# Cumulative log-decays of an RWKV-7 chunk by VectorE transposes and scans instead of TensorE products

## The chip, the core and the metric

One core of one Trainium2 chip runs the kernel. The metric is the device time of one execution in microseconds; a kernel's time is the median over its runs. Engines are TensorE (PE in the profile, its weight loads PEld), VectorE (DVE), ScalarE (ACT), GpSimd (POOL) and SyncE (SP), whose queue issues nearly all DMA transfers.

## The reference

An RWKV-7 recurrence feeds a two-layer MLP with exact GELU.

```python
B, H, S, D = 4, 8, 768, 40                    # r, k, v, w, a, b: (B, H, S, D) float32
for t in range(S):
    y[:, :, t] = einsum('bhd,bhde->bhe', r_t, state)
    Sa = einsum('bhde,bhe->bhd', state, a_t)
    state = state * w_t[:, :, None, :] - outer(Sa, b_t) + outer(v_t, k_t)
x = y.transpose(0, 2, 1, 3).reshape(3072, 320)
out = gelu_exact(x @ w_in) @ w_out            # w_in 320 x 2048, w_out 2048 x 320, float64 in memory
```

## The kernel before

**Chunks.** The 768 steps are cut into 12 chunks of 64 tokens. In a chunk the recurrence is written with matrix products: the decays enter through cumulative products of `w` along the tokens, which are exponentials of cumulative sums of `log w`. All 32 heads are worked at once, as two halves (`g`) and four pairs (`i` or `n`) on the 128 partitions. Work of several chunks overlaps: while the state of chunk c is computed, the inputs of c+1 are prepared, the MLP of an earlier chunk fills TensorE, and GpSimd inverts a triangular matrix.

**The steps of a chunk**, by the names that stand in the order:

- Loads: `Lw`, `La`, `Lb`, `Lk`, `LV`, `Lr`, with tokens on the partitions, and from the third or fourth chunk on `La`, `Lv`, `Lr`, `Lbt`, `Lkt` in pairs of tokens (`load_pairs`), a form that VectorE's 32x32 transposes (`turn`) bring into the layout with features on the partitions. `Lv` and, for chunk 1, `Lr` load `v_pairs`; `La` and `Lbt` share `a_pairs`, `Lr` and `Lkt` share `r_pairs`.
- Decays: `lg` takes the logarithm of `w` in place (ScalarE). `wT` multiplies it on TensorE by the lower triangular matrix `cum_m` so that cumulative sums come out in a PSUM bank with features on the partitions (32 products; the profile shows 64 records, since every product of float32 operands appears as two). `ew` writes exp of these sums to `wpT`, `en` exp of their negative to `kT`. `cu` and `ec` do the same with tokens on the partitions: `ec` writes exp of the negative sums to `part`, which `sb` (VectorE) multiplies into `b` and `sk` (GpSimd for most chunks) into `k`.
- Preparation: `ta`, `tb`, `tk`, `tv`, `tr` transpose; `sa` multiplies `aT` by `wpT`, `sn` makes `nT` from `b` and `kT`, and `kc` then overwrites `kT` with the scaled `k`. So `kT` holds first `en`'s result and later the operand that `am` reads.
- Small products: `nm`, `am`, `vm` on TensorE, masked by `nk`, `ak`, `vk` on VectorE.
- Block inverse (chunk 0 on TensorE by `qm` steps, the others on GpSimd): `Ns` stores the matrix to `N_blocks` in DRAM, `Nl` loads it to `Nb` in another layout, `ic` is 62 instructions of GpSimd on `W`, `Is` stores to `inv_blocks`, `If` and `Ij` load the result to `Tt` and `T2`; `tc_`, `jm`, `jc`, `km`, `kt0`, `kt1` join the blocks.
- State: `av`, `xm`, `xc0`, `xc1`, `sm`, `sc`, `pk`, `pb`, `oa`, `om`, `od`, `ym`, `yc`, `oc`, `tm`, `tn`. `om` writes the rows for the MLP to `xt`, and `ox` moves some of them between partitions by DMA.
- MLP: `mh` (eight parts) and `ge` (GELU); `pm` and `pc`, or from chunk 3 on seven products `m1` to `m7` of a Strassen form with sums `s1` to `s4`, `e1` to `e6`, then `so` stores.
- At the start the float64 weights are loaded (`Lf`, `Lf5`, `Ls`) and turned into float32 by `cp`, `cm`, `cs`, `ce`, `cv` and, in some units, `cl`, `cn`, `cg` (or `cx`, `cy`). `warm` steps are products without use of their result.

**Order.** Nothing is scheduled by the framework. `order` returns one list of step names, and each engine and each DMA queue works its own instructions in the order of that list, waiting on semaphores where data or buffers ask for it. TensorE's results go through four PSUM tiles of two banks each (`take`, `bank`, `drop`): a step waits until the tile that it takes was dropped and read.

Of the kernel before, what the change touches and what calls it, by code (L numbers as in the profile page):

```python
# [16 lines left out]
def order(chunks, first_seven):  # L17
    return """
        pads_a.1 pads_a.0 Lw.0 Lf.0.1.0 lg.0 warm_set identity sums_mask first_ones.1 warm.4.20 warm_first
        Lf.0.0.0 pads_w.1 bias_set pads_r.0 pads_extra.2 pads_extra.3 first_ones.0 pads_rows.1 pads_w.0  # L20
        pads_extra.0 pads_rows.0 upper_mask pads_r.1 iz.1 pads_extra.1 cm.0 cn.0 wT.0 warm.4.5 cu.0 ec.0 cl.0
        cx.0 ew.0 Lf.1.1.0 Lf.1.0.0 Lb.0 La.0 sb.0 cp.1 tb.0 cp.0 ce.0 sn.0 ta.0 sa.0 nm.0 Lw.1 Lb.1 Lf.2.1.0
        Lf5.0.1 Lf.2.0.0 ce.1 lg.1 cm.1 nk.0 qi cu.1 wT.1 warm.4.29 ec.1 cs.0 cy.0 qt qm.0 cs.1 sb.1 cp.2 cm.2
        La.1 qc.0 Lf5.0.0 Lf.3.0.0 cn.2 ew.1 cl.4 ce.2 cl.2 qz.0 Lf.3.1.0 Lf.0.0.1 ta.1 tb.1 warm.4.7 qm.1 cv.1
        sa.1 cp.3 cm.3 sn.1 cs.2 qc.1 qz.1 qa.1 Lr.0 nm.1 tr.0 warm.4.24 LV.0 Lk.0 cg.2 pads_VR.0 Tt_zero sk.0.p
        nk.1 cm.4 qm.2 tv.0 tk.0 Lf.0.1.1 rc.0 ce.3 cs.3 cp.4 qa.2 cv.3 qc.2 cl.5 cn.4 kc.0 qz.2 qm.3 cm.5 cp.5
        cn.5 ce.5 cs.5 ce.4 vc.0 am.0 vm.0 qz.3 qa.3 ak.0 Lf5.1.1 Lf.2.1.1 Lf.2.0.1 Lf.1.1.1 Lw.2 Lf.1.0.1 Ns.1.1
        Ns.1.0 Lk.1 cg.5 pads_VR.1 cs.4 cg.4 cp.7 cm.7 vk.0 qc.3 lg.2 ce.7 cl.7 cn.7 qm.4 cp.6 qa.4 ql ce.6 cm.6
        sk.1.v cs.7 av.0 Lf5.1.0 Nl.1.1 Lr.2 Nl.1.0 Lr.1 Lf.3.0.1 Lf.3.1.1 LV.1 Ls.1 Lb.2 Ls.0 qx warm.4.8 jm.0
        jc.0 cu.2 km.0 xc0.0 cg.7 cs.6 xc1.0 cp.9 cm.9 kt0.0 ce.9 kt1.0 cs.9 cv.9 tr.2 ec.2 rc.2 sm.0 sc.0.0  # L30
        sc.0.1 tk.1 pk.0 pb.0 cv.6 cp.8 kc.1 ce.8 wT.2 tr.1 om.0.0 om.0.1 od.0.0 od.0.1 cm.8 cm.11 cs.8 cv.8 sb.2
        cp.11 tv.1 rc.1 vc.1 ew.2 am.1 vm.1 ak.1 vk.1 cp.10 oc.0 ce.11 cm.10 cs.11 tm.0 tn.0 tb.2 warm.4.1 ox.0.0
        av.1 ym.1 ce.10 sn.2 yc.1 La.2 ta.2 cs.10 cv.10 cv.11 sa.2 Ls.2 Ls.3 cp.12 cp.13 cm.13 cm.12 LV.2 Ls.5
        xm.1 nm.2 tv.2 ox.0.1 Ls.4 Ls.7 Ls.9 Ls.6 Ls.11 nk.2 Ls.8 ic.1.0.4 ic.1.4.8 ic.1.8.12 ic.1.12.16
        ic.1.16.20 ic.1.20.24 unused.v ic.1.24.28 ic.1.28.31 Ns.2.0 Is.1.0.s ce.12 ce.13 cs.13 cv.13 cp.15 cm.15
        xc0.1 ce.15 vc.2 xc1.1 cs.12 cs.15 cv.12 cv.15 cp.17 cm.17 cm.14 ce.17 cn.14 cl.14 cp.14 ce.14 cs.17
        cv.17 cp.19 cm.19 cs.14 cg.14 ce.19 cs.19 cv.19 cp.21 cm.21 Ns.2.1 Ls.13 Is.1.1.s mh.0.6 mh.0.2 mh.0.3
        ge.0.1 mh.0.0 mh.0.1 mh.0.7 mh.0.4 mh.0.5 cp.16 cm.16 ce.21 cs.21 ge.0.0 cn.16 ce.16 cl.16 cv.21 cp.23
        cm.23 cs.16 ce.23 cs.23 cg.16 cv.23 Ls.15 cm.25 cn.25 cl.25 cm.18 cp.25 ce.25 cp.18 cs.25 iz.2 cg.25
        Nl.2.1 If.1.1 vm.2 Ls.10 If.1.0 Ij.1.1 Ij.1.0 Nl.2.0 Ls.12 vk.2 ce.18 pm.0.0 unused.a ic.2.0.4 ic.2.4.8  # L40
        ic.2.8.12 ic.2.12.16 ic.2.16.20 ic.2.20.24 ic.2.24.28 ic.2.28.31 tc_.1 jm.1 jc.1 km.1 cs.18 cv.18 cp.20
        cm.20 ce.20 cs.20 cv.20 cp.22 Ls.14 Lk.2 Lw.3 kt1.1 unused.r kt0.1 ce.22 ge.0.2 cs.22 cm.22 cv.22 ge.0.3
        cp.24 sk.2.v pm.0.1 sm.1 warm.4.0 tk.2 sc.1.1 sc.1.0 pk.1 pb.1 lg.3 kc.2 oa.1.1 oa.1.0 od.1.0 om.1.1
        cm.24 od.1.1 cu.3 ec.3 ce.24 cs.24 om.1.0 cv.24 wT.3 am.2 ak.2 La.3 Lr.3 Lv.3 Lb.3 pm.0.2 tm.1 ew.3 oc.1
        tn.1 av.2 ym.2 yc.2 pm.0.3 ta.3 tr.3 sa.3 sb.3 pc.0.0 pc.0.1 tb.3 xm.2 ox.1.1 Lw.4 ox.1.0 sn.3 nm.3 Lk.3
        so.0.1 tv.3 nk.3 Is.2.0.s Is.2.1.s Ns.3.1 Ns.3.0 sk.3.v Lk.4 Nl.3.1 If.2.0 If.2.1 Ij.2.0 Nl.3.0 Ij.2.1
        mh.1.6 mh.1.4 mh.1.7 ge.1.3 xc0.2 mh.1.5 lg.4 ge.1.2 mh.1.0 mh.1.1 ge.1.0 xc1.2 mh.1.2 tc_.2 jm.2 jc.2
        tk.3 km.2 mh.1.3 kc.3 kt1.2 kt0.2 ge.1.1 sm.2 Lv.4 La.4 sc.2.0 pk.2 wT.4 sc.2.1 ta.4 pb.2 oa.2.0 oa.2.1
        om.2.1 od.2.1 od.2.0 om.2.0 Lr.4 Lbt.4 Lb.5 pm.1.0 am.3 vm.3 ew.4 en.4 oc.2 tb.4 tr.4 sn.4 ak.3 vk.3 sa.4
        pm.1.1 pm.1.3 tm.2 pc.1.1 LV.3 ox.2.1 so.0.0 ox.2.0 cu.4 nm.4 pm.1.2 nk.4 iz.3 ic.3.0.4 ic.3.4.8  # L50
        ic.3.8.12 ic.3.12.16 ic.3.16.20 ic.3.20.24 ic.3.24.28 ic.3.28.31 Is.3.1.p Is.3.0.p ec.4 sk.4.p iz.4
        so.1.1 Lkt.4 tk.4 kc.4 pc.1.0 Ns.4.1 Ns.4.0 Lb.4 Nl.4.1 Nl.4.0 If.3.1 La.5 If.3.0 Ij.3.1 tc_.3 tn.2
        mh.2.6 mh.2.7 mh.2.4 ge.2.3 mh.2.5 ge.2.2 av.3 ym.3 yc.3 mh.2.2 mh.2.3 jm.3 xm.3 ge.2.1 Lw.5 Ij.3.0 jc.3
        km.3 xc0.3 kt0.3 tv.4 xc1.3 ta.5 kt1.3 mh.2.0 mh.2.1 sm.3 Lr.5 ge.2.0 so.1.0 Lbt.5 tr.5 vm.4 vk.4 sb.4
        sc.3.0 sc.3.1 tb.5 pm.2.0 am.4 pk.3 pb.3 ak.4 oa.3.0 oa.3.1 om.3.1 ws.0 om.3.0 od.3.1 od.3.0 lg.5 wT.5
        en.5 sn.5 ew.5 sa.5 Lkt.5 Lv.5 LV.5 La.6 LV.4 ox.3.1 pm.2.1 pm.2.2 tm.3 nm.5 pm.2.3 nk.5 pc.2.1 pc.2.0
        oc.3 tn.3 av.4 ym.4 yc.4 ic.4.0.4 ic.4.4.8 ic.4.8.12 ic.4.12.16 ic.4.16.20 ic.4.20.24 ic.4.24.28
        ic.4.28.31 Is.4.1.p Is.4.0.p ox.3.0 Ij.4.1 If.4.1 If.4.0 Ns.5.1 so.2.1 Ij.4.0 mh.3.0 cu.5 xm.4 tv.5 tk.5
        kc.5 tc_.4 ec.5 jm.4 mh.3.1 jc.4 xc0.4 km.4 kt0.4 ge.3.0 mh.3.6 mh.3.7 Ns.5.0 so.2.0 Nl.5.1 xc1.4 Nl.5.0
        Lw.6 Lr.6 ge.3.3 lg.6 kt1.4 ta.6 sm.4 sc.4.0 ws.3 Lv.6 Lbt.6 sc.4.1 tr.6 mh.3.2 pk.4 pb.4 mh.3.4 mh.3.5  # L60
        mh.3.3 ws.1 oa.4.0 oa.4.1 om.4.1 om.4.0 Lkt.6 iz.5 ic.5.0.4 ic.5.4.8 ic.5.8.12 ic.5.12.16 ic.5.16.20
        ic.5.20.24 ic.5.24.28 ic.5.28.31 Is.5.1.p Is.5.0.p ge.3.1 ge.3.2 vm.5 wT.6 am.5 ox.4.1 m1.3 m2.3 vk.5
        s1.3 ws.2 od.4.0 ak.5 en.6 e1.3 s2.3 od.4.1 tk.6 oc.4 ew.6 e2.3 tb.6 m5.3 m6.3 e4.3 s3.3 tm.4 tn.4 e3.3
        av.5 ym.5 yc.5 sn.6 s4.3 kc.6 sb.5 sa.6 m3.3 m7.3 m4.3 e5.3 e6.3 nm.6 nk.6 xm.5 cu.6 Lb.6 ox.4.0 La.7
        Lk.5 Lr.7 sk.5.p If.5.1 ec.6 mh.4.0 If.5.0 so.3.1 Ns.6.1 Ij.5.0 tr.7 xc1.5 tv.6 ta.7 tc_.5 Ij.5.1 Ns.6.0
        Nl.6.1 Nl.6.0 Lbt.7 mh.4.2 mh.4.1 ge.4.0 mh.4.3 jm.5 mh.4.4 mh.4.5 jc.5 xc0.5 km.5 ge.4.2 kt0.5 ge.4.1
        kt1.5 mh.4.6 sm.5 vm.6 sc.5.1 sc.5.0 vk.6 mh.4.7 ge.4.3 s1.4 pk.5 pb.5 LV.6 Lw.7 Lk.6 Lv.7 Lkt.7 so.3.0
        m1.4 m2.4 tb.7 oa.5.0 oa.5.1 om.5.0 om.5.1 od.5.0 s2.4 s4.4 tk.7 m5.4 lg.7 e1.4 ox.5.1 am.6 wT.7 m6.4
        e2.4 one_set s3.4 od.5.1 e4.4 ak.6 ew.7 en.7 m3.4 m7.4 tm.5 oc.5 e3.4 tn.5 iz.6 ic.6.0.4 ic.6.4.8
        ic.6.8.12 ic.6.12.16 ic.6.16.20 ic.6.20.24 ic.6.24.28 ic.6.28.31 Is.6.1.p Is.6.0.p sk.6.p m4.4 sn.7 sa.7  # L70
        e5.4 e6.4 nm.7 av.6 ym.6 sb.6 nk.7 tv.7 ox.5.0 Lr.8 tr.8 yc.6 mh.5.4 cu.7 ec.7 Ns.7.0 so.4.1 Ns.7.1
        If.6.1 If.6.0 Ij.6.0 so.4.0 Nl.7.0 xm.6 vm.7 mh.5.5 vk.7 kc.7 xc1.6 tc_.6 mh.5.6 mh.5.7 mh.5.0 ge.5.3
        jm.6 mh.5.1 Ij.6.1 Nl.7.1 ge.5.2 jc.6 xc0.6 km.6 ge.5.0 kt0.6 mh.5.2 kt1.6 sm.6 sc.6.0 sc.6.1 Lw.8 La.8
        ta.8 mh.5.3 Lkt.8 ge.5.1 lg.8 pk.6 pb.6 s1.5 m5.5 s4.5 oa.6.0 oa.6.1 om.6.1 s2.5 wT.8 am.7 m1.5 m2.5
        od.6.0 om.6.0 ak.7 e3.5 e1.5 s3.5 LV.7 Lv.8 Lb.7 Lbt.8 Lk.7 iz.7 ic.7.0.4 ic.7.4.8 ic.7.8.12 ic.7.12.16
        ic.7.16.20 ic.7.20.24 ic.7.24.28 ic.7.28.31 Is.7.1.p Is.7.0.p sk.7.p m6.5 ox.6.1 m3.5 m7.5 tb.8 en.8 sn.8
        e2.5 od.6.1 e4.5 ew.8 oc.6 tm.6 tn.6 sb.7 e5.5 av.7 ym.7 yc.7 m4.5 sa.8 tv.8 e6.5 Lb.8 ox.6.0 LV.8 Lk.8
        La.9 cu.8 vm.8 ec.8 vk.8 xm.7 nm.8 If.7.1 Ij.7.1 Ij.7.0 nk.8 tk.8 xc1.7 kc.8 Ns.8.0 Ns.8.1 If.7.0 Nl.8.1
        Nl.8.0 tc_.7 mh.6.6 mh.6.7 ge.6.3 xc0.7 mh.6.4 mh.6.0 jm.7 mh.6.5 jc.7 km.7 mh.6.1 mh.6.2 kt0.7 ge.6.2
        so.5.1 Lw.9 kt1.7 ta.9 sm.7 sc.7.0 sc.7.1 ge.6.0 lg.9 mh.6.3 cu.9 pk.7 pb.7 ge.6.1 Lr.9 so.5.0 Lbt.9 Lv.9  # L80
        tr.9 s1.6 oa.7.1 sb.8 om.7.1 oa.7.0 m1.6 m2.6 s2.6 s3.6 om.7.0 s4.6 od.7.0 iz.8 sk.8.p ic.8.0.4 ic.8.4.8
# [38 lines left out]
def kernel(  # L120
# [16 lines left out]
    C = 64  # L137
# [1202 lines left out]
```

## Time and profile before

| | before |
|---|---|
| three runs | 690.76, 685.67, 688.01 us, median 688.01 |
| the profiled execution | 684.3 us, its span 682.6 us |
| TensorE products | 652.3 us busy, 96% |
| VectorE | 385.2 us, 56% |
| GpSimd | 377.2 us, 55% |
| ScalarE | 236.9 us, 35% |
| DMA | 74.26 MB in 286043 packets, 265660 of them under 512 bytes |
| granted TensorE clock, mean | 0.989 |

The span runs from the first to the last instruction on the engines. The page cuts it into 40 slices of 17 us and gives the busy tenths of each engine; matmul ends are modelled. A row of a group gives the line, the engine, the operation, the tiles written and read, the shapes and the number of records, then busy time and mean duration in ns, then the time that the engine stood idle just before them and what ended most of it. In an answer by windows the five busy times stand in the order PE, PEld, DVE, ACT, POOL, then the granted clock, the DMA share and GB/s. A row of waits gives who waited for whom: microseconds in total, times, the longest.

### The profile page before, as it was taken

The numbers are of one execution on the slowest core, as the hardware profiler recorded it, in microseconds if no ns is written. First come the engines' busy times: TensorE is split into PE (matmuls) and PEld (weight loads), VectorE is DVE, ScalarE is ACT, GpSimd is POOL, SyncE is SP. The second block draws the span as 40 slices with busy tenths as digits, with TensorE's granted clock in tenths as the row PEclk, the third lists the DMA queues.
The fourth block names the chain that finished last, engine by engine and source line by source line (L and its number), as shares of the span: only waits on it lengthen the run. The fifth ranks groups of instructions, "written<-read, shape, count | busy, mean of one in ns | idle before, by whom it ended". The sixth has DMA issues, their size and how long they took to land.

```text
span 682.6 us, 29596 instructions
## 1 busy us (share of the span) xinstructions
PE 652.3 (96%) x13250; PEld 569.6 (83%) x13250; DVE 385.2 (56%) x483; ACT 236.9 (35%) x313; POOL 377.2 (55%) x796
## 2 busy tenths in 40 slices
PE   8687999999999999999989989999999999999997
PEld 4476887788778778998988988997998998998987
DVE  1868989750833645781852853753952763624403
ACT  4547535526222325322323332432342332132020
POOL 3445854853857705871883874864873863840000
PEclk9987999999999999999999999999999999999999
DMA  9987668758668746458547766656767153140100
GB/s 157 161 163 161 129 165 176 131 97 145 111 127 126 150 82 125 95 102 129 110 83 138 126 118 120 129 95 125 131 123 142 35 100 68 31 71 16 26 15 21
DMA packets 286043, 74.26 MB, mean 109 GB/s; under 512 B 265660, under 2 KB 280796, under 8 KB 285916
## 3 DMA queue, kind: packets, MB, share of 16 engines
q1 hardware_dynamic: 284852, 69.84, 55.2%
q0 software_dynamic: 864, 2.36, 2.0%
q8 instruction: 104, 1.70, 1.1%
q14 instruction: 23, 0.19, 0.1%
q10 hardware_dynamic: 200, 0.16, 0.1%
HBM read 58.69 MB, written 9.70 MB: 100 GB/s over the span
## 4 chain that ended last, share of the span: by engine, by line
PE 62%; POOL 14%; SPq 8%; DMA 6%; DVE 5%; issue 4%; ACT 1%; POOLq 0%; DVEq 0%
PE bank L1185 24%; PE bank L194 17%; PE bank L1224 14%; POOL tmp L873 7%; POOL W L875 6%; PE bank L1301 6%; SPq L417 2%; PE bank L697 1%; DMA w_out_sb<-in_moe_w_in_dram 1%; DMA Nb<-N_blocks 1%; DMA inv_blocks<-W 1%; SPq L522 1%; DVE conv L589 1%; SPq L887 1%; DMA r_pairs<-in_r_dram 1%
## 5 line engine op out<-in xcount | busy, mean ns | idle before, releaser
L1185 PE MATMUL bank<-xt,w_in_sb 64*128 64x256 f32 x1920 | 221.0, 383 | 1.8 <-issue 1.6
L873 POOL TENSOR_TENSOR tmp<-W,Nb 128x126 f32<-128x126 f32 (+22 forms) x341 | 152.7, 448 | 122.5 <-DMA Nb<-N_blocks 96.7
L1185 PEld LDWEIGHTS bank<-xt,w_in_sb 64*128 64x128 f32 x1920 | 185.7, 188 | 25.3 <-issue 4.2
L875 POOL TENSOR_TENSOR W<-W,tmp 128x126 f32<-128x126 f32 (+22 forms) x341 | 155.6, 456 | 26.7
L1190 ACT ACTIVATE gt<-bank 128x1024 f32<-128x1024 f32 x48 | 48.9, 1022 | 139.9 <-PE bank L1185 138.7
L1224 PE MATMUL bank<-w_out_sb,gt 128*128 128x160 f32 x576 | 82.8, 301 | 0.0
L1224 PEld LDWEIGHTS bank<-w_out_sb,gt 128*128 128x128 f32 x576 | 79.1, 190 | 1.3 <-issue 0.3
L1301 PE MATMUL bank<-w_out_sb,gt 128*128 128x320 f32 x192 | 54.9, 439 | 1.4 <-DVE w_out_sb L598 0.8
L1301 PEld LDWEIGHTS bank<-w_out_sb,gt 128*128 128x128 f32 x192 | 35.6, 190 | 16.4 <-DVE w_out_sb L598 1.3
L1062 DVE TENSOR_TENSOR SM<-bank,upper 128x832 f32<-128x832 f32 x24 | 23.7, 1016 | 29.2 <-PE bank L194 29.2
L961 DVE STREAM_TRANSPOSE conv<-Tt 128x512 f32<-128x512 f32 x11 | 7.8, 707 | 43.6 <-DMA Tt<-inv_blocks 43.5
L1112 DVE TENSOR_TENSOR st<-bank,st 128x832 f32<-128x832 f32 (+1 forms) x22 | 20.9, 985 | 16.8 <-PE bank L194 16.8
L1010 DVE COPY Tt<-bank 32x512 f32<-32x512 f32 x9 | 6.2, 689 | 41.6 <-ACT Tt L1010 41.5
L1177 DVE TENSOR_TENSOR os<-os,bank 128x160 f32<-128x160 f32 x36 | 11.5, 318 | 26.8 <-PE bank L1224 18.9
L1224 PE MATMUL bank<-extra,conv 128*128 128x160 f32 x176 | 26.0, 301 | 0.0
L1224 PEld LDWEIGHTS bank<-extra,conv 128*128 128x128 f32 x176 | 24.3, 190 | 0.5
L811 DVE TENSOR_TENSOR VR<-bank,upper 128x1024 f32<-128x1024 f32 x12 | 14.6, 1217 | 15.2 <-PE bank L194 15.1
L1177 DVE TENSOR_TENSOR conv<-gt 128x1024 f32<-128x1024 f32 x9 | 11.3, 1257 | 20.5 <-ACT gt L1190 20.4
L1043 DVE COPY SM<-bank 128x832 f32<-128x832 f32 x10 | 10.1, 1013 | 21.1 <-PE bank L194 21.1
L575 ACT ACTIVATE conv<-conv,rebias 128x320 uint32<-128x320 uint32 (+1 forms) x26 | 15.8, 619 | 18.0 <-DVE conv L568 17.9
L864 POOL MEMSET W<- 128x512 f32 x11 | 5.8, 529 | 29.1 <-DMA inv_blocks<-W 29.1
L1079 ACT COPY st<-bank 128x1024 f32<-128x1024 f32 x11 | 11.1, 1013 | 29.9 <-PE bank L194 29.9
(207 smaller groups left out, 1096.9 us busy)
## 6 DMA issues: line engine op xcount, KB each, us to landing
Nb<-N_blocks SPq DMA_DIRECT2D x22, 256.0 KB
b_rows<-in_b_dram SPq DMA_DIRECT2D x24, 160.0 KB
VR<-in_v_dram SPq DMA_DIRECT2D x24, 160.0 KB
k_rows<-in_k_dram SPq DMA_DIRECT2D x24, 160.0 KB
out_dram<-os SPq DMA_DIRECT2D x48, 80.0 KB
Tt<-inv_blocks SPq DMA_DIRECT2D x44, 64.0 KB
a_pairs<-in_a_dram SPq DMA_DIRECT2D x18, 144.0 KB
r_pairs<-in_r_dram SPq DMA_DIRECT2D x36, 72.0 KB
```

Of the source, the lines that this page charges most:

```text
L194: nc.tensor.matmul(o, lhsT, rhs, start=first, stop=True, skip_group_check=True)
L575: nc.scalar.activation(power, power, ACT.Relu, bias=rebias, scale=8.0)
L811: nc.vector.tensor_tensor(to, pt, upper.unsqueeze(1).to_broadcast([P, NBL, C]), ALU.mult)
L873: nc.gpsimd.tensor_tensor(t, W[:, :rows, j:j + 1].to_broadcast([P, rows, rest]), Nb[:, j:j + 1, j + 1:].to_broadcast([P, rows, rest]), ALU ...
L875: nc.gpsimd.tensor_tensor(W[:, :rows, j + 1:], W[:, :rows, j + 1:], t, ALU.add)
L1062: nc.vector.tensor_tensor(SM[:, g], pair_of(f"S{c}_", g).rearrange("p x i c -> p i x c"), pass_upper.unsqueeze(1).unsqueeze(1).to_broadcas ...
L1112: nc.vector.tensor_tensor(to, pair_of(f"QY{c}_", g)[:, :, :, cols], to, ALU.add)
L1177: nc.vector.tensor_tensor(to, one_, other, how)
L1185: nc.tensor.matmul(ph[:, x, s], w_in_sb[half(x), kt, p * P:(p + 1) * P], xt[half(x), kt], start=kt == 0, stop=kt == NK - 1)
L1190: nc.scalar.activation(gt[:, 4 * q:4 * q + 4].rearrange("p (x s) t -> p x s t", x=2), bank(f"ph{c}_{q}").rearrange("p x (s t) -> p x s t", ...
L1224: nc.tensor.matmul(po[:, n, :DM // 2], l_[:, f], r_[:, f], start=f == 0, stop=f == NF // 2 - 1)
L1301: nc.tensor.matmul(po[:, g, :DM], gt[:, f, g * P:(g + 1) * P], w_out_sb[:, f], start=f == 0, stop=f == NF - 1)
```

## The change

For chunks 4 to 11, `wT` and its PSUM tile are gone. A new step `Lwt` loads `w` a second time, in pairs, into `v_pairs`; `tw` transposes it on VectorE into `kT`; `lt` takes the logarithm there on ScalarE; `pw` replaces it with running sums by four VectorE scans of 256 columns. Each scan multiplies the running value by `onward` before adding the next logarithm; `onward` is 1, and 0 at the first token of each 64, so that the sum starts again. `ew` reads the sums from `kT`, and `en` takes exp of their negative in place. `Lw`, `lg`, `cu` and `ec` stay. `onward` lies in the last 256 columns of `spare`; the unused part of `v_pairs` is set to 1 instead of 0.

The list is another one throughout. It has 16 `warm` steps where there were 8; unit 0 of the weights is converted by `cl`, `cn`, `cg` instead of `cx`, `cy`, and some other units change between the two forms.

```diff
+    onward = spare[:, NBL * C:]
...
+    @step
+    def onward_set():
+        nc.gpsimd.memset(onward, 1.0)
+        nc.gpsimd.memset(onward[:, ::C], 0.0)
...
-            eng.memset(paired[n][x * HP + BL:(x + 1) * HP, :, BW - BL:D + BL], 0.0)
+            eng.memset(paired[n][x * HP + BL:(x + 1) * HP, :, BW - BL:D + BL], 1.0 if n == "v" else 0.0)
...
+    @step
+    def Lwt(c, q="s"):
+        load_pairs(c, w, paired["v"], engine(q), False)
...
-        pt = take(f"wT{c}", 1 if c < NB else 2).rearrange("p e (n t) -> p e n t", t=C)
+        pt = take(f"wT{c}").rearrange("p e (n t) -> p e n t", t=C)
...
+    summed = by_batch(kTs)
+
+    @step
+    def tw(c):
+        turn(summed, paired["v"])
+
+    @step
+    def lt(c):
+        nc.scalar.activation(summed, summed, ACT.Ln)
+
+    @step
+    def pw(c):
+        logs = kTs.rearrange("p g n t -> p (g n t)")
+        n = onward.shape[1]
+        for at in range(0, logs.shape[1], n):
+            nc.vector.tensor_tensor_scan(logs[:, at:at + n], onward, logs[:, at:at + n], 0.0, ALU.mult, ALU.add)
...
         to = wp[:, :, 1:].rearrange("p (g n e) t -> p g e n t", g=G, e=2)
+        log = summed.rearrange("p (e g n) t -> p g e n t", e=2, g=G)
         for g in range(G):
-            nc.scalar.activation(to[:, g], pt[:, ::1 - 2 * g, g * NP:(g + 1) * NP], ACT.Exp)
-        drop(f"wT{c}")
+            nc.scalar.activation(to[:, g], log[:, g], ACT.Exp)
...
     def en(c):
-        pt = bank(f"wT{c}").rearrange("p e (n t) -> p e n t", t=C)
-        to = by_batch(kTs).rearrange("p (e g n) t -> p g e n t", e=2, g=G)
-        for g in range(G):
-            nc.scalar.activation(to[:, g], pt[:, ::1 - 2 * g, g * NP:(g + 1) * NP], ACT.Exp, scale=-1.0)
-        drop(f"wT{c}")
+        nc.scalar.activation(summed, summed, ACT.Exp, scale=-1.0)
```

In the list, the steps around the new ones for chunk 8, before and after:

```diff
-        mh.5.3 Lkt.8 ge.5.1 lg.8 pk.6 pb.6 s1.5 m5.5 s4.5 oa.6.0 oa.6.1 om.6.1 s2.5 wT.8 am.7 m1.5 m2.5
...
-        ic.7.16.20 ic.7.20.24 ic.7.24.28 ic.7.28.31 Is.7.1.p Is.7.0.p sk.7.p m6.5 ox.6.1 m3.5 m7.5 tb.8 en.8 sn.8
-        e2.5 od.6.1 e4.5 ew.8 oc.6 tm.6 tn.6 sb.7 e5.5 av.7 ym.7 yc.7 m4.5 sa.8 tv.8 e6.5 Lb.8 ox.6.0 LV.8 Lk.8
-        La.9 cu.8 vm.8 ec.8 vk.8 xm.7 nm.8 If.7.1 Ij.7.1 Ij.7.0 nk.8 tk.8 xc1.7 kc.8 Ns.8.0 Ns.8.1 If.7.0 Nl.8.1
+        kt0.6 vm.7 s1.5 ta.8 xc1.6 kt1.6 vk.7 sm.6 sc.6.0 sc.6.1 pk.6 am.7 Lkt.8 Lwt.8 Lbt.8 Lw.8 so.4.0 sk.7.p
...
+        tw.8 oa.6.1 ak.7 oa.6.0 om.6.1 om.6.0 s2.5 od.6.1 m5.5 m1.5 m2.5 m6.5 lg.8 e1.5 od.6.0 lt.8 oc.6 Lv.8
+        ox.6.1 tm.6 e3.5 tn.6 s3.5 m3.5 s4.5 m7.5 pw.8 e2.5 e4.5 tk.8 e5.5 av.7 ym.7 m4.5 ew.8 en.8 yc.7 xm.7
+        xc0.7 Lb.8 ox.6.0 mh.6.4 Lr.9 tb.8 sb.7 tv.8 sn.8 e6.5 sa.8 nm.8 If.7.0 If.7.1 xc1.7 kc.8 nk.8 tc_.7 vm.8
```

And the start of SyncE's queue, loads and stores alone:

```diff
-Lw.0 Lf.0.1.0 Lf.0.0.0 Lf.1.1.0 Lf.1.0.0 Lb.0 La.0 Lw.1 Lb.1 Lf.2.1.0 Lf5.0.1 Lf.2.0.0 La.1 Lf5.0.0 Lf.3.0.0 Lf.3.1.0
-Lf.0.0.1 Lr.0 LV.0 Lk.0 Lf.0.1.1 Lf5.1.1 Lf.2.1.1 Lf.2.0.1 Lf.1.1.1 Lw.2 Lf.1.0.1 Ns.1.1 Ns.1.0 Lk.1 Lf5.1.0 Nl.1.1
+Lw.0 Lb.0 La.0 Lf.1.0.0 Lf.0.1.0 Lf.0.1.1 Lf.1.1.0 Lw.1 Lr.0 Lf.0.0.0 Lf.3.1.0 Lf.0.0.1 LV.0 Lf.2.0.0 Lf.3.0.0 La.1
+Lf.2.1.1 Lf5.0.1 Lf.2.1.0 Lk.0 Lb.1 Lr.2 Lf.2.0.1 Lf5.0.0 Lf.3.0.1 Lf.1.0.1 Lf5.1.0 Lk.1 Lf.1.1.1 Lf5.1.1 Lf.3.1.1
+Ns.1.1 Lw.2 LV.1 Ns.1.0 Lr.1 Ls.1 Nl.1.1
```

## The prediction

> **What bounds the kernel now.** I read the page from the top: first the busy shares with the slices, then TensorE's waits, then the stretches in which another engine is full.
>
> ```profile
> span 682.6 us, 29596 instructions
> PE 652.3 (96%) x13250; PEld 569.6 (83%) x13250; DVE 385.2 (56%) x483; ACT 236.9 (35%) x313; POOL 377.2 (55%) x796
> ...
> PE   8687999999999999999989989999999999999997
> ...
> DVE  1868989750833645781852853753952763624403
> ```
>
> TensorE (PE) is at 9 in nearly every slice from the fifth on (68 us); only the first four show gaps. VectorE (DVE) is at half, but in lumps: 8 or 9 in one slice of every three, 1 to 3 between. TensorE's waits after 140 us, by releaser:
>
> ```profile
> PE bank L194 <- ACT part L688: 3.5, 2, 1.8
> PE bank L1185 <- issue: 1.6, 2, 1.4
> PE bank L194 <- issue: 1.3, 3, 0.6
> PE bank L1301 <- issue: 0.7, 1, 0.7
> ```
>
> That is 7.1 us in 540: from there on the time is the sum of the matrix work, and work taken from TensorE comes off the end as long as nothing else becomes late. The two waits on L688 are `ec` (the exponential of `cum`), itself waiting for `part`, which `sk` on GpSimd (POOL) reads behind a whole block inversion. After the second one the granted clock is half for 3.5 us (408.4 to 411.8), and 80 products at L1185 take 10.48 us in the chain where they take 8.84 at 460.99, so 1.6 us more are lost.
>
> What is nearest to taking over is seen in the windows 207 to 235 (chunk 4's inversion) and 262 to 301 (chunk 5's):
>
> ```profile
> 207.00:235.00 28.00, 27.53 (x807) 23.57 (x805) 13.97 (x14) 9.08 (x10) 22.80 (x62) 1.00 0.71 122
> 262.00:301.00 39.00, 39.00 (x746) 36.30 (x742) 29.87 (x32) 15.11 (x19) 33.29 (x62) 1.00 0.56 108
> ```
>
> The same 62 GpSimd instructions (fifth figure) take 22.8 us where VectorE (third figure) is half idle, and 33.3 where it works. Within the second window, 279 to 299, VectorE is busy 18.99 us of 20: that lump is the preparation of the next chunk (`tb`, `sn`, `sa`) together with the Strassen sums.
>
> **What is removed.** `wT` of chunks 4 to 11, 64 records of TensorE each:
>
> ```profile
> L194 PE MATMUL bank<-cum_m,w_tile 64*64 64x64 f32 x704 | 13.0, 219 | 1.1 <-issue 1.1
> L703 DVE STREAM_TRANSPOSE aT<-a_pairs 128x1024 f32<-128x1024 f32 x9 | 11.1, 1236 | 0.5 <-PE bank L194 0.4
> L1177 DVE TENSOR_TENSOR gt<-gt 128x1024 f32<-128x1024 f32 x9 | 12.3, 1367 | 0.0
> L1177 DVE TENSOR_TENSOR os<-os 128x160 f32<-128x160 f32 x27 | 10.2, 380 | 0.4
> ```
>
> 704 records are 11 steps (the one of chunk 1 reads SM), so 13.0 / 11 = 1.18 us a step, and 8 steps are **9.5 us**, all on the engine that sets the end. The bank that each held until `en` and `ew` had read it comes free as well.
>
> **What is added, per chunk.** `tw` is a transpose of 128x1024 on VectorE, 1.24 us. `pw` is four scans of 256 elements (1024 over the 256 columns of `onward`). No row shows a scan. Two inputs in SBUF and one output cost 0.38 us at 160 elements and 1.37 at 1024, which gives 0.49 at 256 and 2.0 for four. The dearest element of VectorE is in L568 at 41.54 us, 1.76 us for 512, or 0.88 at 256 and 3.5 for four. I take 2.0, since those rows have the scan's operands, and keep 2.0 to 3.5. [...] So VectorE gets 3.2 us a chunk (up to 4.7), 26 us over eight, at 56% busy.
>
> ScalarE: `lt` is one activation of 1024, about 1.03 us (L670); `en` becomes one of 1.03 instead of two of 0.60. In the new order its table sets alternate 51 times instead of 39, 12 loads more at 1.28 us. All told some 22 us on an engine at 35%, behind the products. SyncE and DMA: `Lwt` is four transfers a chunk, at 0.49 us of issue (L430) 2 us; 32 x 16 rows in each, 2048 packets a chunk beside the 284852 of this queue that take 55.2% of 16 engines, so 2.7 us of all 16. It stands between `Ns` and `Nl` for chunks 6 and 8, where the queue waits for N_blocks anyway (2.3 us to land at 99.62); if that cover is gone, GpSimd starts those two inversions up to 2.7 us later, and 1.4 to 5.9 us lie between `tc_` and `jm` for chunks 7 to 11. I count nothing for either.
>
> **The longer path.** `nm` now waits for `tw`, `lt`, `pw`, `en`, `sn`, where it waited for `en`, `sn`: 1.24 + 1.03 + 2.0 and up to two table loads, 6.8 us more. All of them write `kT`, so none starts before `am` of the chunk before has read it. What lies between is work that TensorE has in its order from that `am` to `nm`: by the rows' durations (2.3 us for an `mh` or an `m`, 1.0 to 1.7 for the rest) 14, 19, 11, 21, 10, 12, 12 us for chunks 5 to 11 before, and 23, 29, 18, 25, 41, 24, 31 after. The new order spreads them, so I hide the path. Between the end of `sa` and the start of `nm` the timelines now show 4.4, 3.6, 2.6, 2.9, 8.0, 1.0, 3.3 and 2.3 us for chunks 4 to 11. If the order's cover fails, that is what is left, and behind `nm` in TensorE's queue are `xm`, the products of the MLP and, through `nk`, GpSimd's next inversion. I take +2.0 for new waits of this kind, a fifth of a microsecond to half of one a chunk, from 0 to 21 (the rival below).
>
> **The new order at the start.** 16 `warm` steps instead of 8, 1.1 us each, and `cx.0` gone. TensorE idles 15.7 us in the first 60, and the DMA queue is what is full there:
>
> ```profile
> 53.60 0.49 SPq L860 DMA_DIRECT2D Nb<-N_blocks  x1
> ```
>
> This first load for chunk 1's inversion is the 61st issue, so 0.89 us each. In the new order 74 stand ahead of it: 65.9 us, 12 later, and the inversion (62.1 to 95.5 now) ends near 108. Now it is followed by 8.9 us in which its stores wait behind weight loads (95.5 to 104.4), and `jm` starts at 115.62; after, the queue is empty of those, and 108 + 1 + 11.2 (104.4 to 115.6) gives 120. TensorE reaches `jm.1` when `mh.0` (18.4 us), `tv.2` (2.0) and two `pm` steps (9.1) are done; `mh.0` needs `ox.0`, whose last transfer is the 101st issue against the 102nd, so 91 us as now: 91 + 29.5 = 120.5. `sm.1` then starts near 123 with one `vm` (1.1) left for later, against 122.0. I count **+2.0**, from -4 (chunk 0 begins 3 us sooner, its w, b and a being loaded first) to +9 (the warm steps on the path).
>
> **Waits that go.** `sk` of chunks 6 and 7 now stands before the inversion in GpSimd's queue, so `ec` need not wait for it: -3.5, from 0 to -5.1 with the clock.
>
> Sum: 684.3 (the profiled execution's own time, 1.7 around a span of 682.6) - 9.5 + 2.0 + 2.0 - 3.5 = 675.3. That execution lies 3.7 under the median of the three runs (688.0); the like of the median is **679.0**.
>
> **Rivals.**
> *GpSimd takes the gain.* The chain follows GpSimd from 320 to 407 us already. Each scan reads two SBUF operands, and the windows show GpSimd slower beside VectorE; if it stands still for all of `pw`, an inversion is 2 to 3.5 us longer while TensorE arrives 1.2 sooner, against 1.4 to 5.9 between `tc_` and `jm`. Some 1 us a chunk comes back, 8 in all: 687. Against it: `tc_` had 2.2 us or more in seven of the last eight chunks. [...]
> *The preparation is late (slower).* VectorE's lump has 1 us of 20 free. If `tw` and `pw` fall into it with no further cover, `sa` is 1.24 + 2.6 us later (middle of the bounds) and TensorE 1.18 sooner, 5.0 together; over the eight distances above that leaves 0.6 + 1.4 + 2.4 + 2.1 + 0 + 4.0 + 1.7 + 2.7 = 14.9 us of waits, and four of them pass 1.74, the wait that brought the half clock at 408, at 1.6 each. 684.3 - 9.5 + 2.0 + 14.9 + 6.4 = 698, or 702 as a median; it decides from some 4 us a chunk uncovered. Against it: the 18 to 41 us of products put in between.
> *More than the work.* The first 60 us shorten by 4 instead of growing by 2, and no new waits: 671.
>
> **How the numbers follow.** The forecast has 0.52, with 674 to 685 as its own range; GpSimd 0.17; late preparation 0.18; more 0.13. A measurement here can tell about 1%, so 681.1 and 694.9 are the marks. Of the forecast's chance 0.37 lies below 681.1 and 0.15 above; with the 0.13 that is 0.50 faster, with GpSimd's 0.17 it is 0.32 the same, and 0.18 slower. The range, 669 to 696, takes in part of the slower case.
>
> **What would show it.** Right: 192 records left in the `cum_m,w_tile` group, TensorE's waits after 140 us under 10 us, a scan between 0.5 and 0.9 us, no wait for the exponential of `ec` above 1 us. Wrong: `nm` (aT,nT) waiting for VectorE or ScalarE's exponential by a microsecond or more a chunk; `jm` waiting for `tc_`; granted clock below 1 after 70 us; `mh.0` starting after 95 us. Should the last sum be right and the time still 688, GpSimd's 62 instructions will have grown.

## The result and the profile after

Twenty runs each: before 687.74 us median (685.67 to 690.78), after 693.29 (686.02 to 698.57). The ratio is 1.0073, 95% interval 1.0053 to 1.0092: **slower by 0.7%**, where 679.0 was forecast. The profiled execution after took 691.71 us, its span is 689.7. (Runs of one kernel spread by up to 2%; the ratios leave out those more than 1.5% above a kernel's fastest, two of the twenty of after, three of the twelve of `few_products` and four of the twelve of `inverse_3us` among them, and since the profiles of `few_products`, `inverse_first`, `inverse_3us` and `kept_busy` are of longer runs and that of `mended` is of a short one, only waits and the distances between steps, not spans, are read from these.)

The page of after, the lines that answer to those of before, and the slices of the granted clock:

```profile
span 689.7 us, 28676 instructions
PE 654.7 (95%) x12750; PEld 567.9 (82%) x12750; DVE 417.1 (60%) x524; ACT 261.7 (38%) x323; POOL 385.6 (56%) x798
...
PE   7888799999999999999998899999999999999997
...
PEclk9999979999999999998999799999999999999999
```

TensorE executes 500 instructions fewer and yet is busy 2.4 us longer: the clock slices show why, at 7, 8 and 7 where they were at 9 (before had its own 8 and 7 in the first 68 us). The trace puts the half clock (0.50 granted in each stretch) at 86.1 to 96.4, 311.4 to 318.2 and 379.7 to 389.9; before, after 60 us, there was one such stretch of 3.4 us, at 408.4. TensorE's waits after 140 us, with the columns as before:

```profile
PE bank L196 <- DVE conv L987: 4.1, 4, 1.8
PE bank L196 <- DVE aT L748: 3.4, 2, 2.5
PE bank L196 <- DMA T<-inv_blocks: 2.8, 4, 1.0
PE bank L196 <- issue: 2.7, 2, 1.8
PE bank L1327 <- issue: 0.7, 1, 0.7
PE bank L196 <- DVE os L1203: 0.3, 1, 0.3
```

14.0 us instead of 7.1. The waits for `ec` are gone, as forecast. New are `jm` waiting for `tc_` (conv L987), `km` waiting for `Ij` (T), and `nm` waiting for `sa` (aT). The first and second are the last steps of the same thing, GpSimd's block inverse on its way back to TensorE. The chain that ended last says it too; first the line of before, then that of after:

```profile
PE 62%; POOL 14%; SPq 8%; DMA 6%; DVE 5%; issue 4%; ACT 1%; POOLq 0%; DVEq 0%
```

```profile
PE 45%; POOL 20%; DMA 12%; SPq 11%; issue 6%; DVE 4%; ACT 1%; POOLq 0%; DVEq 0%; ACTq 0%
```

TensorE has some 113 us less of this chain (62% of 682.6 against 45% of 689.7). GpSimd, the transfers and SyncE's queue together have some 105 us more (28% against 43%); 9 of the 12% of transfers after are the inverse's own stores and loads. The two groups of the change itself, the products that are left and the scans (shortest, median and longest in ns):

```profile
L196 PE MATMUL bank<-cum_m,w_tile x192: 217/218/268, 9.9 to 139.0; 64*64 64x64 f32 x192
L693 DVE TENSOR_TENSOR_SCAN kT<-spare,kT x32: 651/818/2912, 183.7 to 554.5; 128x256 f32<-128x256 f32 x32
```

**The sum, by the two traces.** `sm.1` starts at 125.3 instead of 122.0: 3.3. From there to the end 564.4 instead of 560.6: 3.8, which is 9.5 for the products that are gone, 6.9 more of waits and 6.8 more lost to the half clock (8.5 of the 17.0 us after 140, against 1.7), or +4.2.

That the half clock is no accident of one execution is seen in the runs. I count (1 - c) of a span at granted clock c as lost, an estimate (20 products of L1211 that took 2.43 us elsewhere took 4.15 at 0.50): the mean over runs is 16.9 us after, and 10.4 to 11.7 in the four sets of runs of before below (without one run of 756.12).

### The profile page after: what moved, and what is told of

It reads as the page before. It is cut to its first block, busy times and chain, and to the rows that moved or that the text cites. A ratio compares the mean times of both kernels' runs of the same rounds, so it can differ in the third digit from the quotient of the medians.

```text
span 689.7 us, 28676 instructions
## 1 busy us (share of the span) xinstructions
PE 654.7 (95%) x12750; PEld 567.9 (82%) x12750; DVE 417.1 (60%) x524; ACT 261.7 (38%) x323; POOL 385.6 (56%) x798
## 4 chain that ended last, share of the span: by engine, by line
PE 45%; POOL 20%; DMA 12%; SPq 11%; issue 6%; DVE 4%; ACT 1%; POOLq 0%; DVEq 0%; ACTq 0%
PE bank L196 16%; PE bank L1250 13%; PE bank L1211 12%; POOL W L901 9%; POOL tmp L899 9%; DMA inv_blocks<-W 4%; DMA Nb<-N_blocks 4%; PE bank L1327 3%; PE bank L723 2%; SPq L913 1%; SPq L1320 1%; SPq L1159 1%; DMA Tt<-inv_blocks 1%; SPq L469 1%; SPq L886 1%
## 5 line engine op out<-in xcount | busy, mean ns | idle before, releaser
L1211 PE MATMUL bank<-xt,w_in_sb 64*128 64x256 f32 x1920 | 223.5, 386 | 0.0
L899 POOL TENSOR_TENSOR tmp<-W,Nb 128x126 f32<-128x126 f32 (+22 forms) x341 | 156.3, 459 | 97.9 <-DMA Nb<-N_blocks 71.5
L1211 PEld LDWEIGHTS bank<-xt,w_in_sb 64*128 64x128 f32 x1920 | 185.5, 190 | 26.8 <-issue 2.3
L901 POOL TENSOR_TENSOR W<-W,tmp 128x126 f32<-128x126 f32 (+22 forms) x341 | 159.1, 466 | 26.7
L987 DVE STREAM_TRANSPOSE conv<-Tt 128x512 f32<-128x512 f32 x11 | 7.8, 710 | 54.5 <-DMA Tt<-inv_blocks 54.5
L761 POOL TENSOR_TENSOR k_rows<-k_rows,part 128x640 f32<-128x640 f32 x8 | 12.5, 1566 | 34.1 <-ACT part L714 22.5
L1138 DVE TENSOR_TENSOR st<-bank,st 128x832 f32<-128x832 f32 (+1 forms) x22 | 21.4, 987 | 10.2 <-PE bank L196 10.1
L693 DVE TENSOR_TENSOR_SCAN kT<-spare,kT 128x256 f32<-128x256 f32 x32 | 25.5, 857 | 3.0 <-ACT kT L686 3.0
L196 PEld LDWEIGHTS bank<-SM,Tt 64*64 64x64 f32 x768 | 19.1, 140 | 5.4 <-issue 4.3
L196 PE MATMUL bank<-SM,Tt 64*64 64x104 f32 x768 | 21.8, 262 | 1.1 <-issue 0.9
```

Source lines behind the costliest of these rows:

```text
L196: nc.tensor.matmul(o, lhsT, rhs, start=first, stop=True, skip_group_check=True)
L693: nc.vector.tensor_tensor_scan(logs[:, at:at + n], onward, logs[:, at:at + n], 0.0, ALU.mult, ALU.add)
L899: nc.gpsimd.tensor_tensor(t, W[:, :rows, j:j + 1].to_broadcast([P, rows, rest]), Nb[:, j:j + 1, j + 1:].to_broadcast([P, rows, rest]), ALU ...
L901: nc.gpsimd.tensor_tensor(W[:, :rows, j + 1:], W[:, :rows, j + 1:], t, ALU.add)
L1138: nc.vector.tensor_tensor(to, pair_of(f"QY{c}_", g)[:, :, :, cols], to, ALU.add)
L1211: nc.tensor.matmul(ph[:, x, s], w_in_sb[half(x), kt, p * P:(p + 1) * P], xt[half(x), kt], start=kt == 0, stop=kt == NK - 1)
```

## The experiments

Each ratio is to runs of the kernel before beside it on the same chip, so medians of different rows need not share a chip; "clock loss" is the mean of (1 - clock) times the run's time (for `inverse_first_busy` without one run of 829.91).

| kernel | median us | ratio to before | 95% interval | clock loss us |
|---|---|---|---|---|
| after | 693.29 | 1.0073 | 1.0053 to 1.0092 | 16.9 |
| new_order_products | 707.52 | 1.0343 | 1.0304 to 1.0383 | 16.8 |
| old_order_scans | 738.13 | 1.0790 | 1.0748 to 1.0832 | 33.5 |
| old_order_scans_2 | 736.92 | 1.0731 | 1.0681 to 1.0781 | 33.7 |
| mended | 692.07 | 1.0081 | 1.0046 to 1.0115 | 15.5 |
| kept_busy | 687.43 | 1.0043 | 1.0017 to 1.0068 | 7.3 |
| few_products | 688.89 | 1.0011 | 0.9978 to 1.0043 | 13.1 |
| no_scans | 686.50 | 0.9993 | 0.9965 to 1.0021 | 14.9 |
| no_extra_load | 689.57 | 1.0047 | 1.0019 to 1.0074 | 15.7 |
| filled | 694.08 | 1.0108 | 1.0071 to 1.0146 | 13.9 |
| before_short_inverse | 681.91 | 0.9928 | 0.9902 to 0.9955 | 9.8 |
| after_short_inverse | 676.73 | 0.9849 | 0.9812 to 0.9887 | 8.2 |
| few_short_inverse | 675.52 | 0.9820 | 0.9776 to 0.9865 | 8.4 |
| inverse_3us | 681.21 | 0.9907 | 0.9877 to 0.9938 | 11.2 |
| inverse_first | 691.43 | 1.0033 | 0.9988 to 1.0079 | 16.5 |
| inverse_first_busy | 698.09 | 1.0150 | 1.0101 to 1.0198 | 16.9 |

The theories: (A) the products removed were worth their time, and the waits and half clocks have special causes at three places; (B) the list is the cause, not the method; (C) the scans or the second load make the preparation late; (D) GpSimd's inverse arrives at its own pace, and what TensorE saves it waits out.

### List and method apart

The list of after with `wT` in place of the four steps, and the list of before with them (some `lg`, `ew`, `en` and `Lv` move along with them):

```diff
 # new_order_products: code of before, list of after
-        Lwt.c tw.c lt.c pw.c
+        wT.c
 # old_order_scans: code of after, list of before
-        wT.c
+        Lwt.c tw.c lt.c pw.c
```

> The new list with the old method: for chunks 4 to 11 the second load, transpose, logarithm and scans are out, and the products with their PSUM tile are back just ahead of the two exponentials. If the scans and their longer path cost what was lost, this is faster than the changed kernel (693) by 5 us or more, though 9.5 us of products are back: 683 to 688. If the new list itself is the worse one, it is slower than the changed kernel by about the products: 698 to 704. If list and method share the loss, 690 to 697.

> The old list with the new method: the products of chunks 4 to 11 are out; the transpose and logarithm stand right behind the kT reader of the chunk before, the scans right ahead of the exponentials, which a list not made for them hides badly. If the new list is what lost the time, 678 to 685, below the kernel before (688) by most of the 9.5 us of products. If the scans' path is what loses it, the old list has less cover (10 to 21 us of products between am and nm), so 693 to 705, with nm waiting for VectorE in most chunks.

Both were worse than any theory had it, the second by over 30 us. In the new list the products cost 2.7% more than the scans do; in the old list the scans cost 7.9% over the products. A list is made for one method, so "method" and "list" are not two terms of a sum, and B as stated falls. In the first of these TensorE's waits after 60 us are 26.4 us, in the second 50.7, against 10.3 before: the old list covers little of the 6 us of `tw`, `lt` and `pw`, and `nm` alone waits 15.2 us for `sa` (four times, the longest 6.2).

> The list of before with the method of after once more; in the first one the product vm of chunks 3 and 10 stood behind the turn of the next chunk's w and so read its sums in place of the keys; here the turn stands behind vm. If that order made the 738 us: 690 to 700. If the list of before leaves the scans and what follows no cover: 730 to 740 again.

736.92: the same. The reason given there was a slip: `vm` reads `late` and `rT`, not the sums. What does differ in the computation of both kernels is that `od.4.1` and `od.6.1` stand behind `ew` of two chunks later and so, by the order of the list, take those decays.

### The three places mended, or filled

```diff
 # mended
-tb.2's Lb.2 behind ox.0.0 ... pw.6 behind Lv.6 ... Nl.6.1 so.3.1 LV.6 Nl.6.0 ... La.8 Ij.6.1
+Lb.2 before Ls.4 ... lt.6 pw.6 ... Nl.6.1 Nl.6.0 so.3.1 LV.6 ... Ij.6.1 La.8
 # kept_busy
+warm.4.40 warm.4.41 warm.4.42 tb.2 ... warm.4.43 warm.4.44 nm.6 ... warm.4.45 warm.4.46 jm.6 ... warm.4.47 km.6
 # filled: the last three moves of mended, the first three warm steps, and
+mh.4.4 before nm.6, mh.4.5 before jc.5, mh.6.5 before nm.8
```

> The changed kernel with four steps moved in its list and nothing else: the load of b for chunk 2 ahead of two weight loads, the scans of chunk 6 directly behind their logarithm, the second half of the load of chunk 6's matrix directly behind the first, and one load of chunk 6's inverse ahead of a load of a. If the loss is waits of this list at 85, 311 and 376 to 385 us and the half clock behind them (9.9 us of waits, 13.7 of clock in the profile), those waits go and the time is 674 to 683, mean clock at 0.985 or above. If the scans or the added traffic load the engines everywhere, the waits come up at other places: 689 to 694.

> The changed kernel with eight more warm products (1.1 us each) in TensorE's queue ahead of the places where it waited: three before tb.2, two before nm.6, two before jm.6, one before km.6. The waits stay as long in sum but hold work. If the half clock behind the waits is a loss of its own, it goes and the time falls by 5 to 12 us, to 681 to 688, mean clock 0.985 or above. If the clock follows from something else, the 8.8 us of work show where no wait covers them: 693 to 700, mean clock as now, 0.975.

> The kernel after, all of its computation, with 9 entries of the list changed: three warm steps before tb.2, pw.6 right behind lt.6, Nl.6.0 before so.3.1, Ij.6.1 before La.8, and three feed-forward products moved into waits (mh.4.4 before nm.6, mh.4.5 before jc.5, mh.6.5 before nm.8). By the theory that the half clock after waits eats the gain: clock 0.985 or more, ratio 0.998 to 1.002. If waits only move to the next place: ratio 1.005 to 1.009 at a clock of 0.976.

`mended` stayed where after was (the intervals overlap). At the mended places its waits are shorter (1.79 us to 0.77 at `jm.6`), and others stand elsewhere: 2.5 us at 258.6, 2.3 at 298.4, 3.8 at 81.9, with 19.7 us of waits after 60 against 19.2. So A, as far as this goes, falls: a wait that is removed at one place comes back at the next. `filled` says the same at 1.0108. `kept_busy` is the instructive one: 8.8 us of products that nobody reads were added, and the ratio did not go up (that it fell is not shown: the two intervals share 1.0053 to 1.0068). Its clock loss is 7.3 us against 16.9. So the half clock is a cost of its own beside the wait that it follows, and products of no use can pay for themselves where TensorE would stand still anyhow.

### The scans, the load, the products

```diff
 # no_scans
-        for at in range(0, logs.shape[1], n):
+        for at in range(0):
 # no_extra_load
-        load_pairs(c, w, paired["v"], engine(q), False)
+        pass
...
-        nc.scalar.activation(summed, summed, ACT.Ln)
+        nc.scalar.activation(summed, summed, ACT.Copy, scale=0.0)
 # few_products: the kernel before with
-        for n in range(G * NP):
+        for n in range(G * NP if c < NB else 1):
... (ew and en read that one block for all heads)
```

> The kernel after without its 32 scans: the logarithms are not summed over time, everything else stands. VectorE loses 25.5 us of work, 3.2 a chunk, and the path to nm is shorter by as much. If the length of the scans makes the waits that cost the gain, the time falls by 5 us or more, to a ratio of 1.000 or less against before, and the clock rises to 0.985. If the waits come from the order of loads and of the inversion, it falls by less than 3 us (ratio 1.003 to 1.008).

> The kernel after without the second load of w: the four transfers of Lwt (480 KB a chunk) are left out, the turn takes what lies in the tile, and the ScalarE instruction that makes the logarithms copies with a factor of 0, so that all sums of these chunks are 0. If the transfers delay others (b, r, blocks of the inverse) and so make TensorE wait, the time falls by 4 us or more (ratio of 1.002 or less). If they only fill idle DMA engines, within 2 us of the kernel after (ratio 1.005 to 1.010).

> The kernel before with its own list; from the fifth chunk on wT makes 4 of its 32 products (those of the first pair of heads) and the two exponentials read that one block for all heads, so the sums of the other heads are left out and 28 x 8 = 224 products of TensorE are gone, 8.3 us by the rows of before; nothing else moves. If TensorE's work is worth its time wherever it is taken away, the time falls by 7 to 10 us, a ratio of 0.986 to 0.990. If what is taken away was cover for other waits, or brings the half clock, it falls by less than 4 us (ratio over 0.994).

The scans cost 0.8% of the time, some 5 us: the interval lies clear of that of after. The second load is not told apart from nothing (1.0047 against 1.0073, overlapping; this kernel also has 46 activation table loads where after has 51). And with **no scans at all** the kernel is no faster than before, though TensorE has 9.5 us less to do, and its clock loss stays at 14.9 us. So C is a part and not the cause. `few_products` shows the loss in its plainest form: nothing added, nothing moved, 8.3 us of TensorE's work left out, and the time did not fall (1.0011, where 0.986 to 0.990 was expected if the work counted; the interval leaves at most 1.5 us of gain). Its waits after 140 us:

```profile
PE bank L201 <- DVE conv L968: 4.5, 3, 2.6
PE bank L201 <- ACT part L695: 3.9, 2, 3.0
PE bank L201 <- DMA T<-inv_blocks: 1.7, 1, 1.7
PE bank L1231 <- DVE gt L1184: 1.5, 1, 1.5
```

With three smaller ones that is 13.5 us, where before has 7.1. The first and third have the same names as after: `jm` for the turned inverse and `km` for `T`. The second is that of before, `ec` for `part`, which `sk` reads on GpSimd behind an inversion.

### The inverse made shorter

```diff
 # *_short_inverse, in ic
-        for j in range(j0, j1):
+        for j in range(j0, j1, 1 if c < NB else 2):
 # inverse_3us, in ic
+            if c >= NB and j % 8 == 7:
+                continue
```

> The kernel before with every second elimination step of GpSimd's inversion left out from the fifth chunk on (ic takes j in steps of 2), so the inverse of these chunks is not complete and ic lasts about 14 us less a chunk; every other instruction stands. If TensorE's work sets the time of before and the inverse arrives just in time, the waits for it are few, 10.3 us in all after 60 us, and the time falls by 0 to 4 us (ratio 0.994 to 1.000). If the inverse sets the time of before too: by 10 us or more (0.985).

> The kernel after with the same steps of GpSimd's inversion left out from the fifth chunk on. If the 9.5 us taken from TensorE turned into waits for the inverse, they are worth their time as soon as the inverse comes earlier: 678 to 682 us, a ratio of 0.988 to 0.993 against before, with no wait of jm for the turned block. If the waits have other causes (the path to nm, loads, the clock by itself): 689 or more, 1.004 to 1.008.

> Both together on the list of before: 4 of wT's 32 products from the fifth chunk on, and every second step of the inversion left out. If the inverse ate the gain of the 224 products: 8 us under the kernel before with the short inverse alone, a ratio of 0.982 to 0.988 against before. If products of TensorE are not worth their time in this list whatever the inverse does: within 3 us of before with the short inverse (0.994 to 1.002).

> The kernel after with its own list; every eighth elimination step (j of 7, 15, 23) of the inversion is left out from the fifth chunk on, some 3 to 4 us of GpSimd a chunk, so the inverse of these chunks is not complete. If the inverse is only 1 to 3 us late in each chunk, as the waits of jm and km in the kernel after say, this brings most of what the half inversion brought: 680 to 685 (0.990 to 0.998). If the gain grows with all that is left out: a quarter of it, 688 to 691 (1.001 to 1.005).

The kernel before gains 4.7 us by the short inverse alone, between the 4 at most and the 10 at least that were expected: it waited for the inverse too, but little. The pairs speak for D. With GpSimd's part halved, the same edits that brought nothing bring most of their work: `few_products` 6.4 us (681.91 to 675.52) of its 8.3, where with the whole inverse it cost 1.8; the change under study 5.2 us (681.91 to 676.73), where with the whole inverse it cost 5.5. There are no scans in the `few` pair, so it is not that idle GpSimd makes scans faster. VectorE as a whole is quicker beside the shorter inversion (383.1 us busy to 375.0 in that pair), and what share of the 6.4 us that has was not separated. The waits of `after_short_inverse` after 140 us, and its clock:

```profile
PE bank L204 <- issue: 3.1, 4, 1.0
PE bank L204 <- DVE conv L995: 1.9, 2, 1.6
PE bank L1219 <- issue: 1.6, 1, 1.6
PE bank L204 <- DVE Tt L1044: 1.0, 1, 1.0
```

```profile
PEclk9977999998999999999999999999999999999999
```

With two of 0.4 us more that is 8.4 us of waits, the longest 1.6, and after 200 us every slice at 9. The half clock went with the waits.

`inverse_3us` says how late the inverse is. It takes 3.8 us from each `ic` (33.9 to 30.1 on average) and brings 1.7% of the 2.2% that the half inversion brought with 16.7 us (33.9 to 17.2). A gain in proportion would have been a quarter. One reason is that most of the 16.7 us never reaches `tc_`: from the end of `nm` to the end of `tc_` there are 60.8 us after, 58.0 in `inverse_3us` and 56.3 in `after_short_inverse`. From the issue of the inverse's last store to that of its first load back (`If`) there are 3.9 us after and 17.2 in `after_short_inverse` (means of chunks 4 to 11), because `If` then stands behind other transfers in SyncE's order. So 2.8 us less on this path, mean a chunk, bring most of the gain: the inverse is late by about that much.

The distances agree on the whole. From the end of `nm` to the end of `tc_`, mean over chunks 4 to 11, the trace has 61.9 us before and 60.8 after (`ic` itself 33.3 and 33.9): the path did not get shorter. From the end of `tc_` to the start of `jm` there were 3.2 us before (0.9 to 5.9); after, 0.8, and in four of eight chunks under 0.4. In `after_short_inverse` it is 3.2 again. In `few_products`, with the list of before, it is 2.5, under 0.2 in two chunks, and the path is longer, 64.2 us; why it grew was not found.

### Bringing the inverse forward with the whole computation

```diff
 # inverse_first
-Ns.8.1 Ns.8.0 Lwt.9 Nl.8.0 so.5.1 Ij.7.0 Ij.7.1 Nl.8.1
+Ns.8.1 Ns.8.0 Nl.8.0 Nl.8.1 Lwt.9 so.5.1 Ij.7.0 Ij.7.1
 (likewise chunks 3, 5, 6, 9; sk.6 inside ic.6; sk.7, sk.9, sk.10 behind Is; Lr.8 behind Nl.7)
 # inverse_first_busy: and three warm steps before tb.2, pw.6 behind lt.6
```

> The kernel after, its whole computation; only the order of transfers and of GpSimd's entries is changed, so that the inverse comes earlier: both Nl of chunks 3, 5, 6, 8 and 9 directly behind the stores they read back (Lwt, LV and so behind them), Lr.8 behind Nl.7, sk.6 inside ic.6, and sk.7, sk.9 and sk.10 behind the stores of their inverse. If the late inverse is the cause, and part of its lateness is this order (Nl to ic 14 us in chunk 8 against 8.8 before), the time falls to 682 to 688, a ratio of 0.993 to 1.002, with a clock of 0.98 or more. If only GpSimd's own 30 us a chunk make it late: 691 to 695 (1.005 to 1.010).

> The same order, with three warm steps (3.3 us of products that nothing reads) in the wait of tb.2 for b_rows, and pw.6 directly behind lt.6. If the half clock after the wait at 85 us costs its 5.1 us in most executions, 2 to 4 us less than without them; if the wait and the half clock at 85 us are hidden by what follows, the same or 1 us more.

From the end of `nm` to `ic` 16.2 us became 12.4, but from the end of `ic` to the end of `tc_` 10.7 became 14.8 (in chunk 8, `If` now stands behind `Nl` of chunk 9 and is issued at 469.2, where `ic` ended at 454.7). What was won ahead of GpSimd was lost behind it, and 1.0033 cannot be told from after, nor from before. Why the three warm steps and `pw.6` made it 1.015 was not found. No kernel with the whole computation was shown to be faster than the one before.

## Why the prediction was wrong

- **The removed products** were sized rightly (192 records left, 9.5 us), and the step that failed is the sentence beside them: that work taken from TensorE comes off the end as long as nothing else becomes late. In this list something else becomes late at once. TensorE at 96% with 7.1 us of waits was read as "TensorE sets the time"; `few_products` and its pair with the short inverse show that TensorE and the inverse are in step: 8.3 us of its work alone brought nothing, and 6.4 us with the inverse shortened. Two of the signs of being wrong that were named came: `jm` waits for `tc_`, and the clock is below 1 after 70 us.
- **New waits, +2.0**, was the term mis-sized: without those of `ec`, 14.0 us remain after 140 where 3.6 stood before, so +10.4. I looked for them at `nm`, where 3.4 us came, and named the hiding work there; the larger part came at `jm` and `km`, for which the sum had nothing.
- **GpSimd takes the gain** was the right rival with the wrong mechanism. I priced it by longer inversions, 1 us a chunk, on the estimate that GpSimd stands still for all of `pw`, which no run shows: in the trace of after its instructions go on beside scans (at 343.4 to 346.4 in 0.68 to 0.70 us each, just behind them in 0.43 to 0.45), and `ic` grew by 0.6. It needed no growth: a path of 61 us that stays, and TensorE's work beside it shorter. Against it stood that `tc_` had 2.2 us or more in seven of the last eight chunks; the trace of before has six (0.9 in chunk 4, 1.4 in chunk 7), and after 0.8 is left on average. Of these 2.4 us, 0.8 go in `few_products` too, by the missing products alone; the rest was not separated.
- **The half clock** had its price only in the rival of late preparation, 1.6 us for each wait over 1.74. After 60 us the stretches are 10.2, 6.8 and 10.2 us long and lost by the same estimate 13.7 us in all, against 1.7; 3.4 to 5.1 each. Of the waits of `ec` in before, the one of 1.76 us at 358.3 has no half clock behind it, only the one of 1.74, so a threshold was not to be had from them.
- **The scans** took 0.82 us (median, 0.86 in the mean) beside the 0.5 of the sum, so 3.4 us a chunk and not 2.0, and `no_scans` shows that about 5 us of the time hang on them. The dearer bound, 3.5, was right; the 2.6 in the rival of late preparation was an estimate that no run shows.
- **Near or right:** the start (`mh.0` at 91.48 for 91, `jm.1` at 122.0 for 120.5, `sm.1` at 125.3 for 123, so 3.3 for the 2.0 of the sum); the waits for `ec`, 3.5 us, gone; the second load at nothing that can be measured.

## What to carry to other kernels

Before work is taken from the busiest engine, leave it out alone, with nothing in its place: if the time stays, another path is in step with it, and an engine at 96% with few waits does not tell you so. Small slacks between a slower engine's delivery and its use (here 3 us of 61) are the budget of a change, and they are read chunk by chunk, not as an average share. Where the matrix engine's clock can drop after short waits, price a wait at its length and at the half clock that may follow: here stretches of 3.4 to 10.2 us at 0.50, of which by estimate half is lost.

## What the runs showed of the hardware

**Half clock after short waits.** Two waits of 1.8 us, 4.4 us apart, with short products between and behind them, stand at a stretch of half clock from 379.7 to 389.9:

```profile
376.21 0.85 PE L196 MATMUL bank<-conv,N 32*32 32x32 f32 x64 [1.79 <-DVE conv L987]
380.59 0.26 PE L196 MATMUL bank<-T,Js 32*32 32x32 f32 x2 [1.76 <-issue]
```

One of 2.49 us at 311.8 had 6.8 us, in which 20 products of L1211 took 4.15 us instead of 2.43:

```profile
311.79 1.99 PE L196 MATMUL bank<-aT,nT 40*64 40x64 f32 x64 [2.49 <-DVE aT L748]
314.71 4.15 PE L1211 MATMUL bank<-xt,w_in_sb 64*128 64x256 f32 x20
```

Not every such wait has one: in `mended`, behind 2.33 us of waiting that end at 298.45, the granted clock is 1.00 from 296 to 304. The stretches inside the runs are about 3.4, 6.8, 10.2 or, in `filled` and `inverse_first`, 13.7 us long. Waits of 1.74 us (before, at 407.3) to 2.93 us (after, at 85.5) stand at such stretches, with small products around them; what brings the half clock was not shown.

**Scans and GpSimd.** A scan of 256 elements takes 0.65 to 0.69 us where GpSimd computes little or nothing beside it (27 of them, in after and `after_short_inverse`) and 0.83 to 0.85 (medians of the two) beside its instructions. The sum of the prediction had 0.5. The longest after, 2.91 us, began at 301.46 inside this group of four, while GpSimd issued its store and then ran `sk`:

```profile
300.31 4.64 DVE L693 TENSOR_TENSOR_SCAN kT<-spare,kT 128x256 f32<-128x256 f32 x4
300.62 1.63 POOL L906 DMA_DIRECT2D inv_blocks<-W  x2 [0.30 <-POOL W L901]
302.21 1.60 POOL L761 TENSOR_TENSOR k_rows<-k_rows,part 128x640 f32<-128x640 f32 x1
```

The first two scans of the group stand beside the store alone and took 0.65 and 0.67 us. The third ended at 304.37, 0.56 us behind `sk`. So did every scan of over 1 us in the traces: two of 1.97 us in `inverse_3us` with no store beside them, two in `inverse_first` and one in `kept_busy`, all 0.55 to 0.56 us behind the end of an `sk`. So `sk` goes with the long scans and the store alone does not, though neither was moved to try it. The wait of `nm` at 311.8 is at the end of that group's path.
